# Linear attention ahead of two expert layers: one PSUM bank for both key-value sums, two for transposed queries

## The chip, the cores and the metric

The kernel runs as one launch on one core of a Trainium2 chip. The metric is the device time of a run in microseconds. The engines are TensorE (PE in the profile, with its weight loads as PEld), VectorE (DVE), ScalarE (ACT), GpSimd (POOL) and SyncE (SP), whose queue here only starts DMAs. They run on their own and wait for one another by semaphores. Each engine takes its instructions in the order in which the program wrote them.

## The reference, cut to what matters

```python
def phi(x):                                   # x: 8 x 8 x 576 x 64, w_phi: 64 x 128
    proj = x @ w_phi
    proj = proj - np.max(np.abs(proj), axis=-1, keepdims=True)
    return np.concatenate([np.exp(proj), np.exp(-proj)], axis=-1)      # 256 features
q_p, k_p = phi(q), phi(k)
kv  = k_p^T v                                  # per head: 256 x 64, summed over 576 positions
z   = sum of k_p over the positions            # per head: 256
out = (q_p @ kv) / (q_p . z + 1e-6)
x   = moe(out)          # gated layer, 4608 x 512 through 1536
y   = moe2(x)           # routed layer, 8 experts
```

The weights of the gated layer arrive as 64-bit floats, which the kernel turns into 32-bit floats by integer operations on their two halves.

## The kernel before, in words

Three stages follow each other: attention (up to about 363 us of the trace), the gated layer (up to about 1290 us) and the routed layer. Only the first and the weight conversion change.

**Units and ticks.** Attention works on 16 units. A unit is four heads, as two pairs (`pr` 0 and 1) of two heads each; the two heads of a pair share the 128 partitions or the columns of a matmul. The 576 positions of the two pairs together make nine blocks of 128, taken in three chunks `j` of three blocks. Block 0 is shared: its lower 64 rows belong to pair 0 and its upper 64 to pair 1. The function `attention` is a loop over ticks `tau`, three for each unit; in each tick it writes the steps of several units in a fixed order. `at(f, tau, off)` runs step `f` for the chunk `tau - off`; `once(f, tau, off, ..)` runs it once for the unit that started `off` ticks before. This order, written by hand, is the order of every engine's queue.

**The steps.** `proj` multiplies a chunk of k or q by `w_phi` into PSUM (`ppk`, `ppq`: two banks each, one buffer each). `shift` on VectorE takes the maximum of the absolute values (L94) and subtracts it (L96), into `kpm` or `qpm`. `k_exp` on ScalarE makes both exponentials `kE` (L102). `kv_mm` (L122) sums v times kE into `kv`. `z_add` on GpSimd adds blocks of kE (L133 to L139), and `z_mm` (L144) sums the rest over the partitions with a matrix of ones. `kv_out` copies the sums to SBUF (`kvf`, L147), `kv_tr` (L153) transposes them and copies them back as `KV` (L154). `q_trL` (L159) and `q_tr` (L172) transpose the shifted queries (`lt`, `qt`), `q_exp` (L181) makes their exponentials `qE`, and `q_num` (L193, `nu`) and `q_den` (L212, `dn`) multiply them with KV; `q_out` (L199) and `den_out` (L217) copy and store the results.

**PSUM.** All eight banks are in use: four for `ppk` and `ppq`, one for pair 0's `kv` and `kt`, one for pair 1's, one for `lt` and `qt`, and one for `nu` and `dn`.

**The conversion.** `to_f32` (L306) loads 512 KB and gives two functions. `one` is three VectorE instructions: clear the sign (L317), clamp (L318), shift and mask (L319). `two` is two more (L322, L323). In attention one conversion of `win` (24 in all) takes two ticks: `one` at the end of a tick's work and `two` at the end of the next. In the gated layer 12 conversions of `wout` are written ahead of the split of each weight chunk, one or two in a pass.

**The hand-over.** `START` and `K_TICKS` say at which ticks the first pieces of the gated layer are written between attention's last ones.

Of the kernel before, what the change touches and what calls it, by code (L numbers as in the profile page):

```python
# [10 lines left out]
F32 = mybir.dt.float32  # L11
# [3 lines left out]
AF = mybir.ActivationFunctionType  # L15
ALU = mybir.AluOpType
# [3 lines left out]
B, H, S, D = 8, 8, 576, 64  # L20
F = 128
N = B * S
DM = H * D
NU = 16
P = 128
# [4 lines left out]
GT = 3  # L30


K_TAGS = ("k", "kpm", "kE", "z", "v")
K_TICKS = 3 * NU + 2


def phi_constants(nc, pool, wphi):
# [9 lines left out]
def attention(kctx, qctx, tc, K, wphi, qT, kT, vT, num_d, den_d, r_d, units=NU, extra=None):  # L47
# [3 lines left out]
    nc = tc.nc  # L51
    V, A, G, PE = nc.vector, nc.scalar, nc.gpsimd, nc.tensor
# [3 lines left out]
    psq = qctx.enter_context(tc.tile_pool(name="psq", bufs=1, space=PSUM, side="right"))  # L56
    ident = K["ident"]
    K["qp"] = qp
    w, ones = phi_constants(nc, qp, wphi)
    X = {}  # L60

    def T(shape, dt, tag, key, bufs):
        pool = kp if tag in K_TAGS else qp
        t = pool.tile([P, *shape], dt, tag=tag, bufs=bufs, name=tag + "_".join(map(str, key)))
        X[(tag, *key)] = t
        return t
# [2 lines left out]
        nc.sync.dma_start(T([GT * P], F32, tag, (u, j), 3), src[u, :, j * GT * P : (j + 1) * GT * P])  # L69

    def load_v(u, j):
        t = T([GT, 2, D], F32, "v", (u, j), 4)
        nc.sync.dma_start(t.rearrange("p n h d -> p (n h d)"), vT[u, :, j * GT * P : (j + 1) * GT * P])

    def proj(tag, u, j):
# [27 lines left out]

    def kv_mm(u, j):

        v, E = X["v", u, j], X["kE", u, j]
        todo = [[(0, t, slice(0, P)) for t in (1, 2)], [(0, 0, slice(0, P)), (0, 1, slice(0, P))], []][j]
        if j == 0:
            todo.insert(0, (0, 0, slice(0, D)))
        else:  # L110
            todo += [(1, t, slice(0, P)) for t in ((2,) if j == 1 else range(GT))]
        if j == 1:
            todo.append((1, None, slice(D, P)))
        for i, (pr, t, r) in enumerate(todo):
            start = (j, i) == (0, 0) or (j, i) == (1, 2)
            stop = (j, i) == (1, 1) or (j, i) == (2, GT - 1)
            if start:
                X["kv", u, pr] = psq.tile([P, 3, P], F32, tag=f"kv{pr}", bufs=1, name=f"kv{u}_{pr}")
            v1, E1 = (X["v", u, 0][r, 0], X["kE", u, 0][r, 0]) if t is None else (v[r, t], E[r, t])
            for hh in range(2):  # L120
                o = X["kv", u, pr][64 * hh : 64 * hh + 64, 0:2].rearrange("p s f -> p (s f)")
                PE.matmul(o, lhsT=v1[:, hh], rhs=E1[:, hh].rearrange("p s f -> p (s f)"), start=start, stop=stop)  # L122

    def z_add(u, pr, i):

        def e(j, t):
            return X["kE", u, j][:, t].rearrange("p h s f -> p (h s f)")

        if i == 0:
            z = T([2, 4 * F], F32, "z", (u, pr), 2)  # L130
            r = slice(64 * pr, 64 * pr + 64)
            a, b = ((0, 1), (0, 2)) if pr == 0 else ((2, 0), (2, 1))
            G.tensor_tensor(z[:, 0], e(*a), e(*b), op=ALU.add)  # L133
            G.tensor_tensor(z[r, 0], z[r, 0], e(0, 0)[r], op=ALU.add)
        else:
            z = X["z", u, pr]
            a, b = ((1, 0), (1, 1)) if pr == 0 else ((1, 2), (2, 2))
            G.tensor_tensor(z[:, 1], e(*a), e(*b), op=ALU.add)
            G.tensor_tensor(z[:, 1], z[:, 0], z[:, 1], op=ALU.add)  # L139

    def z_mm(u, pr):
        z, kv = X.pop(("z", u, pr)), X["kv", u, pr]
        for c in range(4):
            PE.matmul(kv[32 * c : 32 * c + 32, 2], lhsT=ones, rhs=z[:, 1, c * F : (c + 1) * F], start=True, stop=True)  # L144

    def kv_out(u, pr):
        A.activation(T([3, P], F32, "kvf", (u, pr), 2), X.pop(("kv", u, pr)), AF.Copy)  # L147

    def kv_tr(u, pr):
        kt = psq.tile([P, 3, P], F32, tag=f"kv{pr}", bufs=1, name=f"kt{u}_{pr}")  # L150
        f = X.pop(("kvf", u, pr))
        for i in range(3):
            PE.transpose(kt[:, i], f[:, i], ident)  # L153
        A.activation(T([3, P], F32, "KV", (u, pr), 3), kt, AF.Copy)  # L154

    def q_trL(u):
        lt = psq.tile([P, 2, P], F32, tag="qt", bufs=1, name=f"lt{u}")
        for hh in range(2):
            PE.transpose(lt[:, hh], X["qpm", u][:, 0, hh], ident)  # L159
        X["lt", u] = lt  # L160
# [6 lines left out]

    def q_tr(u, h):
        pr, hh = h // 2, h % 2
        tp = psq.tile([P, 4, P], F32, tag="qt", bufs=1, name=f"qt{u}_{h}")  # L170
        for j in range(4):
            PE.transpose(tp[:, j], X["qpm", u][:, 1 + 4 * pr + j, hh], ident)  # L172
        X["qt", u, h] = tp
# [29 lines left out]

    def q_den(u, pr):
        KV = X["KV", u, pr]
        dn = psq.tile([P, 288], F32, tag="nu", bufs=1, name=f"dn{u}_{pr}")
        for s in range(2):
            for c in range(4):
                r = slice(32 * c, 32 * c + 32)
                z = 32 * (2 * (c // 2) + s)  # L210
                e = X["qE", u, 2 * pr + c // 2][:, s, 288 * (c % 2) : 288 * (c % 2) + 288]
                PE.matmul(dn[r], lhsT=KV[:, 2, z : z + 32], rhs=e, start=s == 0, stop=s == 1)  # L212
        X["dn", u, pr] = dn
# [21 lines left out]
    def at(f, tau, off, *pre):  # L235

        u, j = divmod(tau - off, 3)
        if 0 <= u < units:
            f(*pre, u, j)

    def once(f, tau, off, *post):
        u, j = divmod(tau - off, 3)
        if 0 <= u < units and j == 0:
            f(u, *post)

    for tau in range(-2, 3 * units + 6):
        at(load, tau, -2, kT, "k")
        at(load, tau, 0, qT, "q")
        at(load_v, tau, -1)

        once(q_out, tau, 7, 2)
        once(den_out, tau, 6, 0)
        once(den_out, tau, 8, 1)
        once(kv_out, tau, 3, 0)
        once(kv_out, tau, 5, 1)

        once(q_trL, tau, 3)
        once(q_tr, tau, 4, 0)
        once(q_tr, tau, 5, 2)
        once(q_expL, tau, 3)  # L260
        once(q_exp, tau, 4, 0)
        once(q_exp, tau, 5, 2)
        at(proj, tau, 0, "k")
        at(proj, tau, 2, "q")
        at(shift, tau, 0, "k")
        at(shift, tau, 2, "q")
        once(kv_tr, tau, 3, 0)
        once(kv_tr, tau, 5, 1)
        once(q_tr, tau, 4, 1)
        once(q_tr, tau, 5, 3)  # L270
        once(q_exp, tau, 4, 1)
        once(q_exp, tau, 5, 3)
        once(z_add, tau, 1, 0, 0)
        once(z_add, tau, 2, 0, 1)
        once(z_add, tau, 3, 1, 0)
        once(z_add, tau, 3, 1, 1)

        once(q_num, tau, 5, 0)
        once(q_num, tau, 6, 1)
        once(q_num, tau, 7, 3)  # L280
        once(q_out, tau, 5, 0)
        once(q_out, tau, 6, 1)
        once(q_out, tau, 7, 3)
        at(kv_mm, tau, 1)
        once(q_num, tau, 6, 2)
        at(k_exp, tau, 0)

        once(z_mm, tau, 2, 0)
        once(z_mm, tau, 4, 1)
        once(q_den, tau, 5, 0)  # L290
        once(q_den, tau, 7, 1)
        once(lambda u: recip_load(u // 2) if u % 2 and u + 1 < units else None, tau, 9)
        once(lambda u: recip(u // 2) if u % 2 and u + 1 < units else None, tau, 11)
        if extra is not None:
            extra(tau)
        yield tau
# [9 lines left out]
def to_f32(nc, pool, src, dst, name):  # L306

    V = nc.vector
    w = pool.tile([P, 512, 2], I32, tag="dbl", name=f"dbl{name}")
    nc.sync.dma_start(w.rearrange("p a b -> p (a b)"), src.bitcast(I32))  # L310

    lo, hi = w[:, :, 0], w[:, :, 1]
    a = dst.bitcast(I32)
    af = a.bitcast(F32)

    def one():
        V.tensor_scalar(a, hi, 0x7FFFFFFF, None, op0=ALU.bitwise_and)  # L317
        V.tensor_scalar(af, af, 2.0**-15, F64_MAX, op0=ALU.max, op1=ALU.min)  # L318
        V.tensor_scalar(a, a, 3, 0x3FFFFFF8, op0=ALU.logical_shift_left, op1=ALU.bitwise_and)  # L319

    def two():
        V.scalar_tensor_tensor(a, hi, -(1 << 30), a, op0=ALU.bitwise_and, op1=ALU.bitwise_or)  # L322
        V.scalar_tensor_tensor(a, lo, 29, a, op0=ALU.logical_shift_right, op1=ALU.bitwise_or)  # L323

    return one, two
# [879 lines left out]

START = (K_TICKS - 5, K_TICKS, K_TICKS, K_TICKS + 1, K_TICKS + 2)
NAMES = ["qT", "kT", "vT", "wphi", "win", "wout", "wg2", "w1", "w2"]
# [3 lines left out]
def attention__moe__moe2_kernel(ctx, tc, qT, kT, vT, wphi, win, wout, wg2, w1, w2, out):  # L1211
# [29 lines left out]
    with tc.manual_schedule():  # L1241
        main, rows = ffn(fctx, tc, K, num_d, r_d, wos_d, wout, wg2, w1, w2, wlo_d, x2_d, L, free)
        for tau in attention(kctx, qctx, tc, K, wphi, qT, kT, vT, num_d, den_d, r_d, extra=convert):
            if tau == K_TICKS:
                assert not todo and not late
# [34 lines left out]
```

## Time and profile before

| | us |
|---|---|
| median of 3 runs | 1817.92 (1817.77 to 1820.62) |
| profiled execution, its own time | 1814.72 |
| its span, first to last instruction | 1813.0 |
| TensorE busy in the span | 1747.5 (96%) |
| VectorE busy | 1270.3 (70%) |
| ScalarE busy | 577.1 (32%) |
| GpSimd busy | 525.3 (29%) |

The mean granted clock of TensorE is 0.987 of full speed. Matmuls overlap, so that the busy time of TensorE is larger than what its matmuls take one after the other: the distance between the starts of two groups is the better price. A row of the timeline that ends in brackets tells how long the engine had sat idle and what ended it.

### The profile page before, as it was taken

What the parts mean: (1) busy time and instruction counts of PE and PEld (TensorE: products, weight loads), DVE (VectorE), ACT (ScalarE), POOL (GpSimd) and SP (SyncE); (2) the same over time, 40 slices, a digit from 0 to 9 for tenths busy, and PEclk for the clock granted to TensorE, in tenths of its full rate; (3) what the DMA queues carried; (4) which work ended last, traced back from release to release, by engine and by line L of the source; (5) the groups of instructions that cost most, each with busy time, mean ns of one, the idle gap of its engine ahead of it and who ended that gap; (6) DMA issues with size and microseconds to landing.
All of it is one profiled execution on the core that took longest, in us unless ns stands there. A gap on an engine that the chain in (4) does not pass through costs nothing.

```text
span 1813.0 us, 32696 instructions
## 1 busy us (share of the span) xinstructions
PE 1747.5 (96%) x11900; PEld 1477.1 (81%) x11900; DVE 1270.3 (70%) x2999; ACT 577.1 (32%) x1112; POOL 525.3 (29%) x461
## 2 busy tenths in 40 slices
PE   7999999899999999999999999999989999999997
PEld 5666656577999999999999999997677889878886
DVE  7999998788768567686776855736757776777410
ACT  4666666622122222222222221111132333233331
POOL 5555555444122223222233221001112211210221
PEclk8999999999999999999999999999989999999999
DMA  4545444375666676666677664201364554465652
GB/s 141 165 150 160 142 142 144 116 245 186 224 230 225 220 238 218 235 220 221 219 243 231 201 227 147 79 1 40 126 198 148 198 195 166 158 198 162 213 171 80
DMA packets 174289, 318.30 MB, mean 176 GB/s; under 512 B 22704, under 2 KB 53680, under 8 KB 174000
## 3 DMA queue, kind: packets, MB, share of 16 engines
q1 hardware_dynamic: 144624, 254.33, 44.1%
q10 hardware_dynamic: 23616, 43.00, 6.3%
q0 software_dynamic: 5888, 18.88, 3.0%
q8 instruction: 94, 1.54, 0.3%
q14 instruction: 67, 0.55, 0.1%
HBM read 244.53 MB, written 71.60 MB: 174 GB/s over the span
## 4 chain that ended last, share of the span: by engine, by line
PE 69%; DVE 4%; DMA 1%; issue 1%; ACT 0%; SPq 0%; POOLq 0%; DVEq 0%; ACTq 0%
PE pg L398 30%; PE acc L420 15%; PE hp L1080 12%; PE yp L1114 8%; PE yr L1101 1%; PE tp L1053 1%; PE cnt L801 1%; DVE cmp L780 1%; DMA rb<-r_d 0%; DMA xg<-x_d,idx 0%; PE lg L454 0%; PE warm L670 0%; PE num_ix L996 0%; DVE oa L987 0%; DMA wos_d<-wh 0%
## 5 line engine op out<-in xcount | busy, mean ns | idle before, releaser
L398 PE MATMUL pg<-xl,wh 128*128 128x384 f32 x1152 | 389.3, 338 | 0.0
L398 PE MATMUL pg<-xh,wl 128*128 128x384 f32 x1152 | 388.0, 337 | 0.0
L398 PE MATMUL pg<-xh,wh 128*128 128x384 f32 x1152 | 386.8, 336 | 0.0
L547 POOL TENSOR_TENSOR el<-er,eh 128x512 fp32r<-128x512 f32 x128 | 183.0, 1429 | 467.9 <-ACT eh L546 410.8
L401 ACT ACTIVATE sg<-pg 128x384 f32<-128x384 f32 x144 | 70.6, 490 | 535.1 <-PE pg L398 510.1
L407 DVE TENSOR_TENSOR sg<-sg,pg 128x384 f32<-128x384 f32 x132 | 72.9, 552 | 239.0 <-PE pg L398 234.4
L398 PEld LDWEIGHTS pg<-xh,wh 128*128 128x128 f32 x1152 | 217.0, 188 | 7.7 <-issue 0.9
L398 PEld LDWEIGHTS pg<-xh,wl 128*128 128x128 f32 x1152 | 215.9, 187 | 5.3
L398 PEld LDWEIGHTS pg<-xl,wh 128*128 128x128 f32 x1152 | 216.4, 188 | 0.0
L478 DVE SCALAR_TENSOR_TENSOR junk<-x,wg 128x512 f32<-128x512 f32 x240 | 194.5, 810 | 5.6
L420 PE MATMUL acc<-wh,gh 128*128 128x512 f32 x396 | 159.6, 403 | 4.7 <-DVE gh L414 2.5
L420 PE MATMUL acc<-wl,gh 128*128 128x512 f32 x396 | 157.8, 398 | 2.2 <-POOL wl L436 2.2
L420 PE MATMUL acc<-wh,gl 128*128 128x512 f32 x396 | 158.3, 400 | 1.3 <-DVE gl L415 1.2
L1114 PE MATMUL yp<-wh,hh 128*128 128x512 f32 x256 | 108.1, 422 | 0.0
L546 ACT ACTIVATE eh<-er 128x512 fp32r<-128x512 f32 x128 | 81.0, 633 | 73.5 <-POOL el L547 41.2
L1114 PE MATMUL yp<-wl,hh 128*128 128x512 f32 x256 | 100.1, 391 | 0.0
L1114 PE MATMUL yp<-wh,hl 128*128 128x512 f32 x256 | 100.1, 391 | 0.0
L1087 DVE SCALAR_TENSOR_TENSOR hl<-hp,hh 128x288 fp32r<-128x288 f32 (+1 forms) x128 | 54.0, 422 | 60.2 <-ACT hh L1085 60.0
L1080 PE MATMUL hp<-xhT,wh 128*128 128x288 f32 x512 | 93.9, 305 | 0.8 <-ACT xhT L1055 0.8
L1080 PE MATMUL hp<-xhT,wl 128*128 128x288 f32 x512 | 94.3, 301 | 0.0
L420 PEld LDWEIGHTS acc<-wh,gl 128*128 128x128 f32 x396 | 75.2, 190 | 21.4 <-DVE gl L415 3.8
L420 PEld LDWEIGHTS acc<-wh,gh 128*128 128x128 f32 x396 | 75.3, 190 | 17.9 <-issue 3.5
(261 smaller groups left out, 3278.8 us busy)
## 6 DMA issues: line engine op xcount, KB each, us to landing
er<-in_w_dram SPq DMA_DIRECT2D x128, 256.0 KB
wlo_d<-el ACTq DMA_DIRECT2D x128, 256.0 KB
wr<-in_w_dram SPq DMA_DIRECT2D x128, 256.0 KB
wl<-wlo_d SPq DMA_DIRECT2D x128, 256.0 KB
wh<-wos_d SPq DMA_DIRECT2D x120, 256.0 KB
wl<-wos_d SPq DMA_DIRECT2D x120, 256.0 KB
dbli<-in_win_dram SPq DMA_DIRECT2D x24, 512.0 KB
k<-in_kT_dram SPq DMA_DIRECT2D x48, 192.0 KB
```

What stands on the lines that cost most here:

```text
L398: PE.matmul(pg, lhsT=a[:, cc], rhs=b, start=c == 0 and j == 0, stop=c == 3 and j == 2)
L401: A.activation(T([TB], F32, "sg", (g,)), X.pop(("pg", g, 0)), AF.Sigmoid)
L407: V.tensor_tensor(u, sg, X.pop(("pg", g, 1)), op=ALU.mult)
L420: PE.matmul(X["acc", i][t], lhsT=a[:, c], rhs=b, start=f == 0 and j == 0, stop=f == NF - 1 and j == 2)
L478: V.scalar_tensor_tensor(junk, x, 1.0, X["wg"][:, e], op0=ALU.mult, op1=ALU.mult, accum_out=out)
L546: A.activation(h, r, AF.Copy)
L547: G.tensor_tensor(tile("el", F32R, k - 1, 3), r, h.bitcast(F32), op=ALU.subtract)
L780: V.tensor_tensor(t[:, c], d[:, c, None, :].to_broadcast([P, NC // 4, NT, 2]), K["it2"][:, None, 0:P:4].to_broadcast([P, NC // 4, NT, 2]), ...
L801: PE.matmul(cnt[:, : 4 * E8], lhsT=eq[:, c // 2 : c // 2 + 2].rearrange("p c t b -> p (c t b)"), rhs=oh[:, c : c + 4].rearrange("p c e -> ...
L1080: PE.matmul(hp, lhsT=x[:, cc], rhs=y[:, c, s], start=c == 0 and j == 0, stop=c == 3 and j == 2)
L1087: V.scalar_tensor_tensor(hl[:, s], hs, 0.0, hh[:, s].bitcast(F32), op0=ALU.max, op1=ALU.subtract)
L1114: PE.matmul(yp, lhsT=x[:, cc], rhs=y, start=f == 0 and j == 0, stop=f == 7 and j == 2)
```

## The change

- Both pairs' key-value sums share one bank (`kv`), one after the other. Pair 1's sum is no longer begun in chunk 1: `kv_mm` for chunk 2 does all of it, out of v and kE of all three chunks, so that v is kept in 6 buffers and not 4.
- The bank that this frees gives `lt` and `qt` two buffers. Pair 0's `dn` is put there too, and no longer waits for the bank of `nu`.
- The transpositions stand together: `kv_tr`, then both `q_tr` of the pair. The queries' projection comes one tick earlier (offset 1, not 2), the rest of the queries' work and pair 1's sums follow one tick earlier, and `K_TICKS` is one less.
- `z_add` no longer adds its two partial sums on GpSimd: three additions a pair, not four. `z_mm` adds them in PSUM, with eight matmuls a pair, not four.
- The sign is cleared on ScalarE, as an absolute value (new L310, `AF.Abs`), not on VectorE. VectorE's next instruction waits for it.

```diff
-K_TICKS = 3 * NU + 2
+K_TICKS = 3 * NU + 1
...
+        pr = j // 2
+        full, half = slice(0, P), slice(pr * D, pr * D + D)
+        todo = [(0, 0, half)]
+        todo += [[(0, t, full) for t in (1, 2)], [(1, t, full) for t in (0, 1)], [(1, 2, full)] + [(2, t, full) for t in range(3)]][j]
+        if j == 1:
+            todo.pop(0)
...
+            X["kv", u, pr] = psq.tile([P, 3, P], F32, tag="kv", bufs=1, name=f"kv{u}_{pr}")
...
-            G.tensor_tensor(z[:, 1], e(*a), e(*b), op=ALU.add)
-            G.tensor_tensor(z[:, 1], z[:, 0], z[:, 1], op=ALU.add)
...
-        for c in range(4):
-            PE.matmul(kv[32 * c : 32 * c + 32, 2], lhsT=ones, rhs=z[:, 1, c * F : (c + 1) * F], start=True, stop=True)
+        for i in range(2):
+            for c in range(4):
+                o = kv[32 * c : 32 * c + 32, 2]
+                PE.matmul(o, lhsT=ones, rhs=z[:, i, c * F : (c + 1) * F], start=i == 0, stop=i == 1)
...
-        tp = psq.tile([P, 4, P], F32, tag="qt", bufs=1, name=f"qt{u}_{h}")
+        tp = psq.tile([P, 4, P], F32, tag="qt", bufs=2, name=f"qt{u}_{h}")
...
-        dn = psq.tile([P, 288], F32, tag="nu", bufs=1, name=f"dn{u}_{pr}")
+        tag, bufs = ("nu", 1) if pr else ("qt", 2)
+        dn = psq.tile([P, 288], F32, tag=tag, bufs=bufs, name=f"dn{u}_{pr}")
...
-        at(proj, tau, 2, "q")
+        at(proj, tau, 1, "q")
...
-        V.tensor_scalar(a, hi, 0x7FFFFFFF, None, op0=ALU.bitwise_and)
+        nc.scalar.activation(af, hi.bitcast(F32), AF.Abs)
```

In the rows below a name carries unit and part: `qt2_3` is the fourth transposition of unit 2, `kE3_1` is chunk 1 of unit 3, `win0_2` a weight chunk.

On TensorE, before, from the end of one tick into the next, around the transposition of pair 1's sums of unit 2:

```order
L172 MATMUL qt2_2_921<-ident_66,qpm2_691 128x128 x4
L81 MATMUL ppk3_2_930<-wphi2_160,k3_2_747 128x128 x6
L81 MATMUL ppq3_0_937<-wphi2_160,q3_0_749 128x128 x6
L153 MATMUL kt2_1_952<-ident_66,kvf2_1_919 128x128 x3
L172 MATMUL qt2_3_958<-ident_66,qpm2_691 128x128 x4
```

and now:

```order
L120 MATMUL kv2_1_859<-kE2_2_764,v2_2_625 64x256 x6
L141 MATMUL kv2_1_859<-z2_1_848,ones_158 32x128 x8
L81 MATMUL ppk3_1_892<-wphi2_160,k3_1_707 128x128 x6
L81 MATMUL ppq3_0_899<-wphi2_160,q3_0_709 128x128 x6
L150 MATMUL kt2_1_914<-ident_66,kvf2_1_890 128x128 x3
L169 MATMUL qt2_2_920<-ident_66,qpm2_648 128x128 x4
L169 MATMUL qt2_3_925<-ident_66,qpm2_648 128x128 x4
```

The transposition that stood ahead of the projections stands behind them, and only the two projections stand between the last matmuls on the sums and their transposition.

On VectorE, before, over two ticks (a conversion's first three and last two instructions behind the shifts):

```order
L96 TENSOR_TENSOR qpm2_691<-ppq2_1_774,mq_2_1_785 128x2x3x128
L317 TENSOR_SCALAR win0_2_121<-dbli2_0_745 128x512
L318 TENSOR_SCALAR win0_2_121<-win0_2_121 128x512
L319 TENSOR_SCALAR win0_2_121<-win0_2_121 128x512
L94 TENSOR_REDUCE mk_3_1_854<-ppk3_1_840 128x6
```

and now:

```order
L96 TENSOR_TENSOR qpm2_648<-ppq2_2_810,mq_2_2_821 128x2x3x128
L311 TENSOR_SCALAR win0_2_121<-win0_2_121 128x512
L312 TENSOR_SCALAR win0_2_121<-win0_2_121 128x512
L94 TENSOR_REDUCE mk_3_1_906<-ppk3_1_892 128x6
L96 TENSOR_TENSOR kpm3_1_907<-ppk3_1_892,mk_3_1_906 128x2x3x128
```

One of the three is gone, and L311 now waits for ScalarE.

On ScalarE, before, from the end of a tick's exponentials to the next copy of the sums:

```order
L199 ACTIVATE nums2_0_969<-nu2_0_970 128x288
L102 ACTIVATE kE3_2_985<-kpm3_2_945 128x6x128 x2
L217 ACTIVATE den2_0_1010<-dn2_0_992 128x288
L147 ACTIVATE kvf3_0_1016<-kv3_0_880 128x384
L166 ACTIVATE eL3_1021<-lt3_1018 128x256 x2
```

and now:

```order
L102 ACTIVATE kE3_0_870<-kpm3_0_818 128x6x128 x2
L310 ACTIVATE win0_2_121<-dbli2_0_786 128x512
L144 ACTIVATE kvf2_1_890<-kv2_1_859 128x384
L151 ACTIVATE KV2_1_918<-kt2_1_914 128x384
L178 ACTIVATE qE2_2_930<-qt2_2_920 128x512 x2
```

The absolute value stands right behind the exponentials of the chunk and ahead of the copy of the sums.

## Rows read from the trace of the kernel before

**Rows 1.** Stretches: us, length, busy of PE, PEld, DVE, ACT, POOL, clock, DMA.

```profile
100.00:150.00 50.00, 50.00 (x542) 31.74 (x542) 44.73 (x54) 33.54 (x66) 30.94 (x30) 1.00 0.50 152
150.00:200.00 50.00, 46.04 (x478) 29.37 (x474) 48.65 (x46) 29.67 (x58) 27.96 (x28) 0.97 0.47 145
```

**Rows 2.** Timeline of PE, once a unit: start us, us, instruction.

```profile
41.92 0.44 PE L159 MATMUL lt<-ident,qpm 128*128 128x128 f32 x2
...
81.69 0.44 PE L159 MATMUL lt<-ident,qpm 128*128 128x128 f32 x2
...
104.95 0.44 PE L159 MATMUL lt<-ident,qpm 128*128 128x128 f32 x2
...
124.83 0.44 PE L159 MATMUL lt<-ident,qpm 128*128 128x128 f32 x2
...
336.05 0.44 PE L159 MATMUL lt<-ident,qpm 128*128 128x128 f32 x2
```

**Rows 3.** Waits of PE from 50 to 340 us: total, times, longest.

```profile
PE qt L172 <- DVE qpm L96: 9.5, 7, 2.2
```

**Rows 4.** Timeline of PE at three places where it had waited.

```profile
25.82 0.69 PE L172 MATMUL qt<-ident,qpm 128*128 128x128 f32 x2 [2.84 <-DVE qpm L96]
...
195.09 0.44 PE L172 MATMUL qt<-ident,qpm 128*128 128x128 f32 x2 [2.17 <-DVE qpm L96]
195.46 1.34 PE L81 MATMUL ppk<-wphi,k 64*128 64x128 f32 x12
```

**Rows 5.** Timeline of DVE: a conversion undisturbed, then in a late tick.

```profile
122.83 0.42 DVE L317 TENSOR_SCALAR win<-dbli 128x512 int32<-128x512 int32 x1
...
164.16 1.53 DVE L317 TENSOR_SCALAR win<-dbli 128x512 int32<-128x512 int32 x1
165.72 1.38 DVE L318 TENSOR_SCALAR win<-win 128x512 f32<-128x512 f32 x1
...
168.43 0.94 DVE L94 TENSOR_REDUCE mk<-ppk 128x6 f32<-128x768 f32 x1
...
171.34 0.96 DVE L96 TENSOR_TENSOR qpm<-ppq,mq 128x768 f32<-128x768 f32 x1
```

**Rows 6.** Timeline of POOL beside the late conversion.

```profile
165.48 1.33 POOL L134 TENSOR_TENSOR z<-z,kE 64x512 f32<-64x512 f32 x1
```

**Rows 7.** Timeline of PE in a unit without waits.

```profile
116.14 0.43 PE L144 MATMUL kv<-z,ones 128*32 128x128 f32 x8
116.38 1.15 PE L212 MATMUL dn<-qE,KV 128*32 128x288 f32 x16
117.47 0.66 PE L172 MATMUL qt<-ident,qpm 128*128 128x128 f32 x4
118.06 0.94 PE L81 MATMUL ppk<-wphi,k 64*128 64x128 f32 x12
...
119.59 0.55 PE L153 MATMUL kt<-ident,kvf 128*128 128x128 f32 x3
119.98 0.60 PE L172 MATMUL qt<-ident,qpm 128*128 128x128 f32 x4
120.51 1.19 PE L193 MATMUL nu<-qE,KV 128*64 128x288 f32 x8
```

**Rows 8.** Groups by line and shape, 50 to 340 us: busy, mean ns, idle before.

```profile
L102 ACT ACTIVATE kE<-kpm 128x768 f32<-128x768 f32 x82 | 64.4, 835 | 17.8 <-DVE kpm L96 17.8
...
L317 DVE TENSOR_SCALAR win<-dbli 128x512 int32<-128x512 int32 x21 | 17.7, 841 | 0.0
...
L147 ACT ACTIVATE kvf<-kv 128x384 f32<-128x384 f32 x28 | 13.6, 485 | 0.0
```

**Rows 9.** Group of ACT in the gated layer, 340 to 1290 us.

```profile
L435 ACT ACTIVATE wh<-wo 128x512 fp32r<-128x512 f32 x12 | 7.6, 632 | 62.8 <-issue 41.1 <-DVE wo L323 21.6
```

**Rows 10.** Timeline of PE where attention ends and the gated layer goes on.

```profile
360.24 1.19 PE L193 MATMUL nu<-qE,KV 128*64 128x288 f32 x8 [1.40 <-ACT nums L199]
...
363.05 0.45 PE L398 MATMUL pg<-xh,wh 128*128 128x384 f32 x1
```

More of the change, by code (lines that the diff above doesn't have):

```diff
@@ L71, in load_v @@
     def load_v(u, j):
-        t = T([GT, 2, D], F32, "v", (u, j), 4)
+        t = T([GT, 2, D], F32, "v", (u, j), 6)
         nc.sync.dma_start(t.rearrange("p n h d -> p (n h d)"), vT[u, :, j * GT * P : (j + 1) * GT * P])
@@ L104, in kv_mm @@
     def kv_mm(u, j):
[L106 to L109, printed above, removed]
-        else:
[L111 to L119, printed above, removed]
+        pr = j // 2
[4 more added lines that the diff above has]
+            todo.pop(0)
+        else:
+            X["kv", u, pr] = psq.tile([P, 3, P], F32, tag="kv", bufs=1, name=f"kv{u}_{pr}")
+        for i, (g, t, r) in enumerate(todo):
+            v, E = X["v", u, g][r, t], X["kE", u, g][r, t]
             for hh in range(2):
                 o = X["kv", u, pr][64 * hh : 64 * hh + 64, 0:2].rearrange("p s f -> p (s f)")
-                PE.matmul(o, lhsT=v1[:, hh], rhs=E1[:, hh].rearrange("p s f -> p (s f)"), start=start, stop=stop)
+                e = E[:, hh].rearrange("p s f -> p (s f)")
+                PE.matmul(o, lhsT=v[:, hh], rhs=e, start=j != 1 and i == 0, stop=j > 0 and i == len(todo) - 1)
     def z_add(u, pr, i):
@@ L129, in z_add @@
         if i == 0:
-            z = T([2, 4 * F], F32, "z", (u, pr), 2)
-            r = slice(64 * pr, 64 * pr + 64)
[L132 to L137, printed above, removed]
-            G.tensor_tensor(z[:, 1], e(*a), e(*b), op=ALU.add)
-            G.tensor_tensor(z[:, 1], z[:, 0], z[:, 1], op=ALU.add)
+            T([2, 4 * F], F32, "z", (u, pr), 2)
+        z = X["z", u, pr][:, i]
+        a, b = (((0, 1), (0, 2)), ((1, 0), (1, 1)), ((2, 0), (2, 1)), ((1, 2), (2, 2)))[2 * pr + i]
+        G.tensor_tensor(z, e(*a), e(*b), op=ALU.add)
+        if i == pr:
+            r = slice(64 * pr, 64 * pr + 64)
+            G.tensor_tensor(z[r], z[r], e(0, 0)[r], op=ALU.add)
     def z_mm(u, pr):
         z, kv = X.pop(("z", u, pr)), X["kv", u, pr]
-        for c in range(4):
-            PE.matmul(kv[32 * c : 32 * c + 32, 2], lhsT=ones, rhs=z[:, 1, c * F : (c + 1) * F], start=True, stop=True)
+        for i in range(2):
+            for c in range(4):
+                o = kv[32 * c : 32 * c + 32, 2]
+                PE.matmul(o, lhsT=ones, rhs=z[:, i, c * F : (c + 1) * F], start=i == 0, stop=i == 1)
     def kv_out(u, pr):
@@ L149, in kv_tr @@
     def kv_tr(u, pr):
-        kt = psq.tile([P, 3, P], F32, tag=f"kv{pr}", bufs=1, name=f"kt{u}_{pr}")
+        kt = psq.tile([P, 3, P], F32, tag="kv", bufs=1, name=f"kt{u}_{pr}")
         f = X.pop(("kvf", u, pr))
@@ L156, in q_trL @@
     def q_trL(u):
-        lt = psq.tile([P, 2, P], F32, tag="qt", bufs=1, name=f"lt{u}")
+        lt = psq.tile([P, 2, P], F32, tag="qt", bufs=2, name=f"lt{u}")
         for hh in range(2):
@@ L247, in attention @@
         at(load, tau, -2, kT, "k")
-        at(load, tau, 0, qT, "q")
+        at(load, tau, -1, qT, "q")
         at(load_v, tau, -1)
-        once(q_out, tau, 7, 2)
+        once(kv_out, tau, 3, 0)
+        once(kv_out, tau, 4, 1)
+        once(q_out, tau, 6, 2)
         once(den_out, tau, 6, 0)
         once(den_out, tau, 8, 1)
[L254 to L262, printed above, removed]
         at(proj, tau, 0, "k")
-        at(proj, tau, 2, "q")
+        at(proj, tau, 1, "q")
         at(shift, tau, 0, "k")
-        at(shift, tau, 2, "q")
+        at(shift, tau, 1, "q")
         once(kv_tr, tau, 3, 0)
[L268 to L272, printed above, removed]
+        once(kv_tr, tau, 4, 1)
+        once(q_trL, tau, 2)
+        for h in range(2):
+            once(q_tr, tau, 3, h)
+            once(q_tr, tau, 4, 2 + h)
+        once(q_expL, tau, 2)
+        for h in range(2):
+            once(q_exp, tau, 3, h)
+            once(q_exp, tau, 4, 2 + h)
         once(z_add, tau, 1, 0, 0)
@@ L276, in attention @@
         once(z_add, tau, 3, 1, 1)
[L278 to L283, printed above, removed]
+        for off, i in ((4, 0), (5, 1), (6, 3)):
+            once(q_num, tau, off, i)
+            once(q_out, tau, off, i)
         at(kv_mm, tau, 1)
-        once(q_num, tau, 6, 2)
+        once(q_num, tau, 5, 2)
         at(k_exp, tau, 0)
         once(z_mm, tau, 2, 0)
-        once(z_mm, tau, 4, 1)
+        once(z_mm, tau, 3, 1)
         once(q_den, tau, 5, 0)
```

## The prediction

> **What bounds the kernel now.** I read the stretches of the span first, then TensorE's timeline in attention, then its waits, then VectorE beside GpSimd. From 100 to 150 us TensorE has no idle time and a full clock; from 150 to 200 it is busy for 46.04 of 50 us at 0.97, and VectorE, at 48.65, is then the fuller engine [rows 1]. So attention is bound by TensorE, and in some units by VectorE. The unit's first transposition shows how much: 104.95 to 124.83 is 19.88 us, a unit without waits; 81.69 to 104.95 is 23.26 [rows 2]. From 41.92 to 336.05 are 14 units and 294.1 us; 14 times 19.88 is 278.3, so 15.8 us are lost in the middle of attention. TensorE's waits there are all of one kind, 9.5 us in 7 pieces, for the shifted query of the tick before [rows 3]. The rest is clock: behind the wait at 195.09 twelve projection matmuls take 1.34 us and not 0.94 [rows 4, 7].
>
> Why VectorE is late is seen in one tick. Its four shift instructions take 168.43 to 172.30, 3.87 us. Ahead of them L317 took 1.53 us where the same instruction took 0.42 at 122.83, and L318 took 1.38 [rows 5]. GpSimd's addition ran from 165.48 to 166.81 and L318 ended at 167.10, 0.29 later [rows 5, 6]: the slow form is a wait for GpSimd. With all three instructions slow, a tick costs VectorE 3.87 + 1.53 + 1.4 + 1.4 (L319 taken at L318's price), 8.2 us, against TensorE's 19.88 / 3 = 6.63.
>
> **The change part by part.** The sum goes along TensorE up to the point where the gated layer runs without a break, at 363.05 [rows 10].
>
> *More matmuls for z.* A group of four (eight rows of the trace) moves the next group by 116.38 - 116.14 = 0.24 us [rows 7]. One more per pair is 0.48 a unit, all on the bounding engine. The ends are zero, if the second set hides in the first, and the group's whole 0.43 each, 0.86 a unit. I take 0.48, since the rows follow each other closely on one weight matrix.
>
> *Transpositions together.* Four of them take 118.06 - 117.47 = 0.59 us behind another kind of matmul, and 120.51 - 119.98 = 0.53 behind a transposition [rows 7]. Two groups a unit gain that, 0.12. The key-value matmuls are as many as before, ten blocks a unit, and only move; I cost that at nothing, between a gain and a loss of 0.2 a unit (a switch of kind, 0.06, three times). A unit is then 19.88 + 0.48 - 0.12 = 20.24 us, and 14 are 283.4.
>
> *The sign on ScalarE.* VectorE loses L317, 0.84 us in the mean [rows 8], 24 times in attention. In the late tick 8.2 becomes 3.87 + 2 x 1.4 = 6.7 us, about TensorE's new 20.24 / 3 = 6.75. So the loss that VectorE made should mostly go. But L311 now waits for ScalarE, where the absolute value stands behind the chunk's two exponentials (1.67 us) [rows 8]. Its own price isn't shown; a ScalarE copy of the same 128x512 takes 0.63 [rows 9], the 768-wide exponential 0.84, the 384-wide copy 0.49 [rows 8]. I take 0.63, so ScalarE finishes it 2.3 us after the key shift, when VectorE has just finished the query shift (1.9 us later). That alone costs VectorE 0.4 us a conversion; if ScalarE comes late to the exponentials, more. Queued behind L311 are the next tick's shifts, and TensorE's next projections and ScalarE's exponentials wait for those. What the order gives in return is a longer way: the transposition that TensorE waited at stands behind two projections now, 1.53 us later (119.59 - 118.06) [rows 7]. I leave 2.5 us of stalls in the 14 units, between none and the 15.8 of before, near the low end, because a tick of VectorE fits even with both instructions slow.
>
> By the Trainium skill (SBUF — State Buffer, Who interferes with whom) a VectorE instruction in a two-port mode and a GpSimd instruction lock each other out for a whole instruction, so the absolute value's place would make it worse: GpSimd starts its additions when the exponentials end, just ahead of L311. The trace agrees about the lock, by the 0.29 us above; by that rule alone both instructions would always be slow, and that is the first rival.
>
> *GpSimd.* It loses two of eight additions a unit (1.33 us each by the one shown [rows 6]), 2.7 us, off the path; less of it stands in VectorE's way. I count nothing further.
>
> *Banks.* Pair 1's sums must now wait until ScalarE has copied pair 0's transposed ones out of the one bank. By the new order two groups of transpositions and a `nu` group stand between on TensorE, about 2.2 us (0.53 + 0.53 + 1.19 [rows 7]), against one copy of 0.49 [rows 8]: hidden, if ScalarE is on time. Pair 0's `dn` no longer waits for ScalarE to empty `nu`. Only the new second rival counts these waits.
>
> *The ends.* One tick of depth goes. Behind the last unit's mark 27.0 us pass (363.05 - 336.05) [rows 2, 10]. The query's first transposition, two `nu` groups and part of a `kv` group now stand ahead of it, about 3.1 us of matmuls (0.44 [rows 2], two of 1.19 [rows 7], and 0.3 left to the `kv` group, an estimate), and the waits there (1.40 us at one of them [rows 10]) lose perhaps 1.4: 22.5. The bounds are 27.0 and a whole tick less, 20.4. At the head the same work comes earlier and falls into holes like the 2.84 us at 25.82 [rows 4]; VectorE has one more query shift there (1.9 us) and three L317 fewer (2.5). I take 40.4 for 41.92, between 38 and 44.
>
> *The gated layer.* Twelve conversions lose an L317 on VectorE, and ScalarE has room for them: it sat idle for 62.8 us ahead of the split's copy [rows 9]. Minus 0.5, between a gain of 2 and a loss of 2. The matmuls behind are the same.
>
> *Sum.* 40.4 + 283.4 + 2.5 + 22.5 = 348.8 against 363.05, 14.2 less; with the gated layer 14.7. The profiled execution took 1814.72 (span 1813.0), so 1800.0. The median of the runs shown is 3.2 above that execution, which gives 1803.
>
> **The rivals.**
>
> *VectorE stays late.* If GpSimd meets both instructions of every conversion, each costs about a microsecond more than its undisturbed 0.43, 24 times 1.9 or 46 us of VectorE's time, most of it inside the slack of 6.75 us ticks. If 0.35 us of each conversion reaches TensorE, 8 us of stall stand where I have 2.5: 1809. For it speaks that the starting signal is shared; against it, that GpSimd has a quarter less to add.
>
> *The one bank, and slower than before.* From the last z matmul to the transposition of the sums TensorE has only its two projections, 1.53 us [rows 7]. In that time ScalarE must copy the sums, 0.49, which leaves about 1.0. If ScalarE is then still at exponentials and absolute value (2.3 us), the copy is late by 1.3, TensorE stands, and nothing can fill another bank. At 24 conversions that is 31 us: 1834. It decides from 14.7 / 32 = 0.46 us at each of the 32 pairs. Against it: ScalarE is busy for only 33.5 of 50 us [rows 1], and pair 1's sums of ten blocks are long, so that it should have caught up.
>
> *No change to speak of.* If the second z set costs 0.43 and not 0.24, 16 units lose 6.1 us more, and if the ends gain nothing, 6 more: 1815.
>
> **How the numbers follow.** The forecast has 0.62, the late VectorE 0.17, the bank 0.11, no change 0.10. What a measurement of this kernel can tell from no change is about 0.2%, 3.6 us, so faster is under 1814.3 and slower over 1821.6. Faster: all of the forecast and nearly all of the first rival and a third of the last, 0.82. Same: 0.08. Slower: 0.10. The range goes from 1796 (no stalls, 2.5; head at 38, 2.4; a gated layer with 1.5 more gained) to 1815, the last rival; it leaves out the bank.
>
> **What would show it.** Right: unit marks 20.2 us apart at a clock of 1.00, two z sets 0.48 us long, no wait for the shifted query, the gated layer's second set of matmuls starting near 349 us, an absolute value near 0.63. Wrong: VectorE idle ahead of L311 by over a microsecond with TensorE waiting at a projection one tick later (first rival); TensorE waiting at `kt` for `kvf` or at `kv` for `KV` (second); marks over 20.6 us apart with no waits at all (third).

## The result and the profile after

The changed kernel takes 1799.18 us in the median (1794.65 to 1800.71, six runs) against 1819.03 for the kernel before in the same series: a ratio of 0.9888, 95% interval 0.9873 to 0.9904. The forecast was 1803, inside a range of 1796 to 1815. The profiled execution has a span of 1792.9 us where it was 1813.0, 20.1 less.

The page of the changed kernel, its first lines:

```profile
span 1792.9 us, 33156 instructions
...
PE 1738.4 (97%) x12156; PEld 1476.4 (82%) x12156; DVE 1250.4 (70%) x2963; ACT 593.5 (33%) x1148; POOL 479.5 (27%) x429
```

The same two stretches of attention as in [rows 1], after the change:

```profile
100.00:150.00 50.00, 50.00 (x578) 33.06 (x578) 46.47 (x47) 34.50 (x68) 25.08 (x26) 1.00 0.54 171
150.00:200.00 50.00, 50.00 (x578) 31.54 (x581) 46.82 (x49) 34.58 (x69) 20.78 (x23) 1.00 0.48 159
```

TensorE now has no hole in either, at a full clock. VectorE is nearly as full as before.

The timeline of TensorE with the marks that answer to [rows 2, 10]. The first transposition of a unit no longer opens a tick; the next tick begins 4.87 us behind it:

```profile
34.28 0.44 PE L156 MATMUL lt<-ident,qpm 128*128 128x128 f32 x2
...
39.15 0.94 PE L81 MATMUL ppk<-wphi,k 64*128 64x128 f32 x12
...
54.44 0.44 PE L156 MATMUL lt<-ident,qpm 128*128 128x128 f32 x2
...
316.87 0.44 PE L156 MATMUL lt<-ident,qpm 128*128 128x128 f32 x2
...
321.73 0.94 PE L81 MATMUL ppq<-wphi,q 64*128 64x128 f32 x12
...
342.35 1.19 PE L190 MATMUL nu<-qE,KV 128*64 128x288 f32 x8 [1.40 <-ACT nums L196]
...
346.87 0.44 PE L391 MATMUL pg<-xh,wh 128*128 128x384 f32 x1
```

A unit is 20.16 us long (54.44 - 34.28). The 14 units take 316.87 - 34.28 = 282.6, where they took 294.1: 11.5 less. The head, up to the tick of 41.92 in [rows 2], ends at 39.15: 2.8 less. At 346.87 the second set of the gated layer's matmuls (about 2.08 us) is done already, which began at 363.05 in [rows 10]; its counterpart is 344.8, so up to there 18.3 us are gained, and 18.3 - 11.5 - 2.8 = 4.0 of them in the tail. The other 1.8 of the 20.1 come later, in the gated layer's first 100 us, where the conversions of `wout` are. A second profile of the changed kernel, from a later run, gains as much up to there within 0.6 us, and yet its span is 1797.9 us: it loses 5 us in later stages that the change does not touch. So a gain is better read from such marks than from two spans.

Of the waits of TensorE from 50 to 340 us, that for the shifted query [rows 3] is gone. All but the last row here belong to the tail, behind the last unit's mark; the last one, for a load, makes one unit 20.52 us long:

```profile
PE nu L190 <- ACT den L215: 1.2, 1, 1.2
PE dn L210 <- ACT nums L196: 0.9, 1, 0.9
PE kt L150 <- ACT kvf L144: 0.7, 1, 0.7
PE nu L190 <- ACT nums L196: 0.5, 1, 0.5
PE ppk L81 <- DMA k<-in_kT_dram: 0.3, 1, 0.3
```

In a unit, against [rows 7], the groups that the change made longer or put together:

```profile
98.07 0.64 PE L141 MATMUL kv<-z,ones 128*32 128x128 f32 x16
98.53 1.15 PE L210 MATMUL dn<-qE,KV 128*32 128x288 f32 x16
...
101.15 0.55 PE L150 MATMUL kt<-ident,kvf 128*128 128x128 f32 x3
101.53 1.04 PE L169 MATMUL qt<-ident,qpm 128*128 128x128 f32 x8
102.50 1.19 PE L190 MATMUL nu<-qE,KV 128*64 128x288 f32 x8
```

Two z sets move the next group by 0.46 us (98.53 - 98.07), where one moved it by 0.24, and eight transpositions take 0.97 (102.50 - 101.53), where two groups of four took 0.59 and 0.53.

VectorE's and ScalarE's groups of the conversion, 50 to 340 us, against L317 in [rows 8]:

```profile
L316 DVE SCALAR_TENSOR_TENSOR win<-dbli,win 128x512 int32<-128x512 int32 x21 | 26.9, 1282 | 0.7
L315 DVE SCALAR_TENSOR_TENSOR win<-dbli,win 128x512 int32<-128x512 int32 x21 | 26.4, 1258 | 0.0
L312 DVE TENSOR_SCALAR win<-win 128x512 int32<-128x512 int32 x21 | 22.3, 1061 | 0.7
L311 DVE TENSOR_SCALAR win<-win 128x512 f32<-128x512 f32 x21 | 20.5, 978 | 17.2 <-ACT win L310 17.2
...
L310 ACT ACTIVATE win<-dbli 128x512 f32<-128x512 f32 x21 | 14.4, 686 | 0.9 <-DMA dbli<-in_win_dram 0.9
```

The four that are left still take 4.6 us, about twice what they take undisturbed (0.43, 0.43, 0.68 and 0.69 in the timeline): the clamp is slow in 19 of the 21 conversions and the shift in 14, each time beside an addition on GpSimd. VectorE also stands 17.2 us for the absolute value, which takes 0.69. It isn't seen in the time, since TensorE is the one that is never idle.

### The profile page after: what moved, and what is told of

It reads as the page before. It is cut to its first block, busy times and chain, and to the rows that moved or that the text cites. A ratio compares the mean times of both kernels' runs of the same rounds, so it can differ in the third digit from the quotient of the medians.

```text
span 1792.9 us, 33156 instructions
## 1 busy us (share of the span) xinstructions
PE 1738.4 (97%) x12156; PEld 1476.4 (82%) x12156; DVE 1250.4 (70%) x2963; ACT 593.5 (33%) x1148; POOL 479.5 (27%) x429
## 4 chain that ended last, share of the span: by engine, by line
PE 67%; DVE 6%; DMA 2%; issue 2%; ACT 1%; SPq 0%; POOLq 0%; POOL 0%; ACTq 0%; DVEq 0%
PE pg L391 29%; PE acc L413 14%; PE hp L1073 12%; PE yp L1107 8%; PE yr L1094 1%; PE tp L1046 1%; DMA rb<-r_d 1%; PE cnt L794 1%; DVE cmp L773 1%; DVE junk L471 1%; DVE oa L980 0%; DVE xn L364 0%; DMA xg<-x_d,idx 0%; PE lg L447 0%; DVE xh L367 0%
## 5 line engine op out<-in xcount | busy, mean ns | idle before, releaser
L471 DVE SCALAR_TENSOR_TENSOR junk<-x,wg 128x512 f32<-128x512 f32 x240 | 200.1, 834 | 5.5
L131 POOL TENSOR_TENSOR z<-kE 128x512 f32<-128x512 f32 x48 | 63.9, 1331 | 143.1 <-ACT kE L102 143.1
```

Source lines behind the costliest of these rows:

```text
L131: G.tensor_tensor(z, e(*a), e(*b), op=ALU.add)
L471: V.scalar_tensor_tensor(junk, x, 1.0, X["wg"][:, e], op0=ALU.mult, op1=ALU.mult, accum_out=out)
```

## The experiments

Theory A was the prediction's: TensorE waits where VectorE, held up by GpSimd, needs more than TensorE's tick, and the three parts (sign, z sums, order) each help a little. Its rivals were that the new order alone did it, and that GpSimd's relief alone did. So the change was cut into three: S, the sign on ScalarE; Z, the z sums on TensorE; O, the banks and the order. All eight combinations were measured, each against the kernel before on its own chip. A mark is the start of a unit's first transposition (`lt`), 0 to 15; the mean unit is the time from mark 1 to mark 15, in one profile, divided by 14.

| parts | ratio to before | 95% interval | mean unit, us |
|---|---|---|---|
| none | 1 | | 21.01 |
| S | 0.9976 | 0.9959 to 0.9994 | 20.87 |
| Z | 0.9935 | 0.9916 to 0.9955 | 20.33 |
| S, Z | 0.9915 | 0.9887 to 0.9943 | 20.33 |
| O | 1.0088 | 1.0059 to 1.0118 | 22.38 |
| S, O | 0.9944 | 0.9925 to 0.9963 | 21.00 |
| Z, O | 0.9990 | 0.9974 to 1.0006 | 21.39 |
| S, Z, O (the change) | 0.9888 | 0.9873 to 0.9904 | 20.19 |

### The change without one part, and the order alone

Without Z, on the changed kernel:

```diff
-        z = X["z", u, pr][:, i]
...
+            G.tensor_tensor(z[:, 1], z[:, 0], z[:, 1], op=ALU.add)
...
-        for i in range(2):
-            for c in range(4):
+        for c in range(4):
```

> The changed kernel with the partial z sums added on GpSimd again (four additions and four matmuls a pair). Theory A (VectorE was late because of GpSimd and L317; the z matmuls are a price paid on TensorE, 0.46 us a unit): units shorten from 20.16 to about 19.70 us where nothing waits, but GpSimd's two more additions a unit bring back about 3 us of TensorE's waits; about 1795. Rival B (the new order alone removed the waits): 19.70 in every unit, no waits, 16 x 0.46 = 7.4 us less: about 1792. If GpSimd's relief is what mattered: waits of 10 us or more come back and it is slower than the changed kernel, about 1803.

It takes 1806.1 us, 0.9944. From the third on the units alternate between 20.56 and 21.77. Waits of TensorE, 50 to 340 us:

```profile
PE ppq L81 <- DVE qpm L96: 9.6, 13, 1.3
PE ppk L81 <- DVE kpm L96: 1.8, 6, 0.3
```

That is the third of the three expectations, GpSimd's relief, and not mine. Without S:

```diff
-        nc.scalar.activation(af, hi.bitcast(F32), AF.Abs)
+        V.tensor_scalar(a, hi, 0x7FFFFFFF, None, op0=ALU.bitwise_and)
```

> The changed kernel with the sign cleared on VectorE again. Theory A: a tick with three slow instructions takes VectorE 8.2 us against TensorE's 6.72, so TensorE waits again, 5 to 8 us in the 14 units, now at the query's projection: about 1805. Rival B (order alone): no waits, units of 20.16, about 1799 as the changed kernel.

It takes 1813.36, 0.9990, with units of mostly 21.35 and 21.56. TensorE waits where theory A said:

```profile
PE ppq L81 <- DVE qpm L96: 8.2, 13, 0.8
```

But the loss is over twice what I had put down: 17 us in the 14 units (21.39 against 20.16) and not 5 to 8. With both edits, O alone:

> Only banks and order of the change; the sign on VectorE and the z sums on GpSimd as before. Theory A: units of 19.70 where nothing waits, but 8 to 12 us of waits and slow clock, so about 1800. Rival B: 19.70 throughout, about 1792, faster than the changed kernel.

It takes 1831.8, 1.0088. Both theories are far off: the order alone makes the kernel slower. The stretch from 50 to 340 us, TensorE's waits, and the conversion's groups on VectorE:

```profile
50.00:340.00 290.00, 266.92 (x2795) 165.23 (x2794) 282.07 (x264) 168.32 (x336) 160.46 (x156) 1.00 0.44 141
```

```profile
PE ppq L81 <- DVE qpm L96: 19.2, 24, 0.9
```

```profile
L316 DVE SCALAR_TENSOR_TENSOR win<-dbli,win 128x512 int32<-128x512 int32 x20 | 33.9, 1694 | 0.0
L317 DVE SCALAR_TENSOR_TENSOR win<-dbli,win 128x512 int32<-128x512 int32 x20 | 33.0, 1649 | 0.7
L311 DVE TENSOR_SCALAR win<-dbli 128x512 int32<-128x512 int32 x19 | 28.7, 1511 | 0.0
L312 DVE TENSOR_SCALAR win<-win 128x512 f32<-128x512 f32 x19 | 26.3, 1385 | 0.7
L313 DVE TENSOR_SCALAR win<-win 128x512 int32<-128x512 int32 x19 | 13.9, 729 | 0.7
```

VectorE is busy for 282 of 290 us: it bounds every unit. A conversion costs it 1.69 + 1.65 + 1.51 + 1.39 + 0.73 = 7.0 us. The timelines suggest why it does not get out of this state. VectorE, then GpSimd:

```profile
205.48 0.96 DVE L96 TENSOR_TENSOR qpm<-ppq,mq 128x768 f32<-128x768 f32 x1
206.36 1.47 DVE L311 TENSOR_SCALAR win<-dbli 128x512 int32<-128x512 int32 x1
207.86 1.38 DVE L312 TENSOR_SCALAR win<-win 128x512 f32<-128x512 f32 x1
```

```profile
206.28 1.27 POOL L131 TENSOR_TENSOR z<-kE 128x512 f32<-128x512 f32 x1 [2.02 <-ACT kE L102]
```

Where VectorE is late, ScalarE waits for its key shift, makes the exponentials (1.67 us by [rows 8]) and so releases GpSimd just when VectorE has done the query shift (1.9 us behind the key shift) and comes to the conversion: GpSimd's addition starts 0.08 us ahead of L311, and the conversion is late again. A late VectorE thus keeps itself late. Where TensorE or ScalarE is the late one, the exponentials and GpSimd start later, and part of the conversion is through by then, as in this unit of the kernel before, where L317 (0.42) and L318 are short:

```profile
136.49 0.43 DVE L318 TENSOR_SCALAR win<-win 128x512 f32<-128x512 f32 x1
136.50 1.54 POOL L138 TENSOR_TENSOR z<-kE 128x512 f32<-128x512 f32 x1 [2.58 <-ACT kE L102]
```

That this is the whole reason why O alone is slower, and not only what its trace shows, was not tried by itself.

### One or two parts in the old order

The edits are those of the change's diff: its last two lines for S, the lines of `z_add` and `z_mm` for Z.

> The kernel before with the sign on ScalarE alone. Theory A (in attention TensorE waits wherever VectorE, held up by GpSimd, needs more than TensorE's tick; each of the two reliefs counts): L317 was up to 1.5 of VectorE's 8.2 us, so 22 to 23 us units become 20 to 21, the mean about 20.3 with 4 to 7 us of waits left, about 1807. Rival (GpSimd's relief is the one that counts): units as before, within 0.2% of before.

S takes 1809.87, 0.9976. TensorE still waits 8.8 us for the shifted query, in ten pieces where it was 9.5 in seven [rows 3]:

```profile
PE qt L172 <- DVE qpm L96: 8.8, 10, 1.6
```

Neither expectation fits well. The time moved the way theory A says, but less; a mean unit of 20.87 and 8.8 us of waits are nearer to the rival's "as before" than to theory A's 20.3 and 4 to 7.

> The kernel before with the partial z sums added on TensorE alone. Theory A: two GpSimd additions fewer a unit leave VectorE half of its late ticks, so the 15.8 us of lost time fall to about 8, and the matmuls cost 16 x 0.46 = 7.4: within 0.2% of before, about 1815. Rival (GpSimd's relief is the one that counts): no waits, units of 20.3, about 1805.

Z takes 1802.64, 0.9935: the rival. Every unit is 20.32 or 20.33. TensorE waits for nothing from VectorE; the longest of its waits in the same stretch, and the conversion's groups:

```profile
PE qt L171 <- ACT qE L180: 0.7, 2, 0.4
```

```profile
L322 DVE SCALAR_TENSOR_TENSOR win<-dbli,win 128x512 int32<-128x512 int32 x21 | 29.8, 1418 | 0.7
L318 DVE TENSOR_SCALAR win<-win 128x512 int32<-128x512 int32 x21 | 26.1, 1243 | 0.7
L321 DVE SCALAR_TENSOR_TENSOR win<-dbli,win 128x512 int32<-128x512 int32 x21 | 17.3, 824 | 0.0
L317 DVE TENSOR_SCALAR win<-win 128x512 f32<-128x512 f32 x21 | 13.3, 632 | 0.7
L316 DVE TENSOR_SCALAR win<-dbli 128x512 int32<-128x512 int32 x21 | 9.4, 448 | 1.5 <-DMA dbli<-in_win_dram 1.5
```

A conversion is 4.6 us here, with the sign still on VectorE: L316, the sign, takes 0.45 where it took 0.84 [rows 8]. So the z sums on TensorE, which I had entered as a pure cost with nothing in return, remove all of TensorE's waits for VectorE in the old order. They do two things at once: GpSimd has two additions fewer, and TensorE's unit is 0.45 us longer, which is room for VectorE. No run parts the two.

> The kernel before with the sign on ScalarE and the z sums on TensorE, in the old order and banks. Theory A: VectorE is relieved, so most of the 15.8 us of lost time goes (12 to 13), while the z matmuls cost 7 more: about 1813. Rival B (the order did it): waits stay at 9 us or more and the z matmuls are added: about 1826.

S with Z takes 1800.85, 0.9915, faster than either theory said, and its units are those of Z alone. The order adds 0.14 us a unit and the ends: in the profiles the gated layer's first split of `wout` on ScalarE starts at 364.7 us without the order and at 356.2 with it, 8.5 earlier, of which 2.0 are units. The times bear this out less sharply, since the two intervals in the table overlap.

### One bank for the queries again

```diff
-            X["kv", u, pr] = psq.tile([P, 3, P], F32, tag="kv", bufs=1, name=f"kv{u}_{pr}")
+            X["kv", u, pr] = psq.tile([P, 3, P], F32, tag=f"kv{pr}", bufs=1, name=f"kv{u}_{pr}")
...
-        tp = psq.tile([P, 4, P], F32, tag="qt", bufs=2, name=f"qt{u}_{h}")
+        tp = psq.tile([P, 4, P], F32, tag="qt", bufs=1, name=f"qt{u}_{h}")
```

and the same for `kt`, `lt` and pair 0's `dn`.

> The changed kernel with two banks for the key-value sums again and one for the transposed queries; the order is the new one. Theory A (the bank pays for transpositions that stand together): each pair's second transposition waits until ScalarE has copied KV and made both exponentials of the first, about 1.2 us, twice a unit: units of about 22.5, about 1838. Rival (VectorE alone sets the units): TensorE's waits there are hidden in nothing but slack, units of 20.2 and about 1799.

It takes 1836.56, 1.0125 (1.0092 to 1.0158), with units of 22.95. Theory A, near its number. TensorE's timeline at such a wait, of which there are 25 from 50 to 340 us, 29.4 us in all:

```profile
202.53 0.60 PE L169 MATMUL qt<-ident,qpm 128*128 128x128 f32 x4
204.30 0.66 PE L169 MATMUL qt<-ident,qpm 128*128 128x128 f32 x4 [1.18 <-ACT qE L178]
```

So the second bank of the queries is what lets transpositions stand together, and one bank for the key-value sums costs nothing that shows. Two banks for the sums in the new order, with two for the queries, would need a ninth bank and weren't tried.

### Half of the z sums, and the sign ahead of the exponentials

Pair 1's partial sums go back to GpSimd, where the addition falls beside VectorE's work on PSUM, and pair 0's stay on TensorE:

```diff
+        if i == pr == 1:
+            G.tensor_tensor(z, X["z", u, 1][:, 0], z, op=ALU.add)
...
-        for i in range(2):
+        for i in range(pr, 2):
...
```

> The changed kernel with pair 1's two partial z sums added on GpSimd (seven additions a unit) and pair 0's on TensorE (twelve z matmuls a unit). Theory A: VectorE reads and writes PSUM while GpSimd does pair 1's last addition, so nothing is held up, and the units take 20.16 - 0.23 = 19.93: about 1795.5, with no waits. Rival (any more GpSimd work holds VectorE up): half of the way to the kernel with all z sums on GpSimd, units of about 20.6, slower than the changed kernel, about 1803.

It takes 1791.77, 0.9885 (0.9851 to 0.9918). The units are 19.94, and from the sixth on every second one 20.1 to 20.2. It was then run beside the changed kernel on one chip:

> The changed kernel itself, as the measure on this chip for the two others. All theories: 0.989 of before, about 1799.

> Pair 1's z sums added on GpSimd, pair 0's on TensorE, once more beside the changed kernel. Theory A (a z set is 0.23 us of a unit that TensorE bounds): 16 x 0.23 = 3.7 less, minus about 1 us for the 0.26 us by which every second unit came longer: 2.5 to 5 us faster than the changed kernel, about 1795. Rival: the same time as the changed kernel within a microsecond, since what TensorE saves comes back as waits.

The changed kernel took 1797.14, 0.9888 (0.9858 to 0.9918), and this one 1794.57, 0.9871 (0.9843 to 0.9898). The units with half of the z sums repeat to 0.03 us; the total differs by 2.6, as theory A has it, but the intervals overlap. For the longer second units the absolute value was written ahead of the chunk's exponentials:

```diff
+        if early is not None:
+            early()
         at(k_exp, tau, 0)
...
```

> As the kernel before it, and the absolute value written ahead of the chunk's exponentials on ScalarE, so that VectorE should not wait for it. Theory A (the 0.26 us in every second unit come from VectorE, which waits for the absolute value behind the exponentials): VectorE's wait of 9.7 us ahead of its clamp goes and all units take 19.93: about 1 us less than the kernel before it. Rival (ScalarE's exponentials then come 0.65 us later in every second tick, and TensorE or GpSimd waits for those): units of 20.1 or more, same or slower.

It takes 1793.57, 0.9855 (0.9827 to 0.9882). All units are 19.93 or 19.94, as theory A said; the time is the same within the noise. VectorE's wait for the absolute value falls from 9.7 us to 5.2 and does not go, but something larger happens. The stretch from 50 to 340 us with the absolute value behind the exponentials (the run before), and ahead of them:

```profile
50.00:340.00 290.00, 285.19 (x3160) 180.84 (x3157) 271.48 (x275) 201.32 (x396) 151.45 (x157) 1.00 0.46 152
```

```profile
50.00:340.00 290.00, 285.33 (x3171) 181.34 (x3170) 223.38 (x276) 200.81 (x398) 149.50 (x157) 1.00 0.47 152
```

VectorE's busy time falls by 48 us, from 271 to 223, though it runs the same instructions. Clamp and shift are now through before the exponentials end and start GpSimd; they bring about 25 of the 48 (0.42 and 0.47 us in the mean, where the run before has 1.04 and 1.06). The conversion's other two instructions bring some 16 more and the small addition to the denominators (`dens`) 6, since they too are slow less often. Clamp and shift on VectorE's timeline:

```profile
104.52 0.43 DVE L320 TENSOR_SCALAR win<-win 128x512 f32<-128x512 f32 x1 [0.62 <-ACT win L316]
104.98 0.43 DVE L321 TENSOR_SCALAR win<-win 128x512 int32<-128x512 int32 x1
```

With that much room, all z sums were put back on GpSimd, with the sign ahead:

> The changed kernel with all z sums added on GpSimd again and the absolute value written ahead of the exponentials. Theory A (clamp and shift meet GpSimd only because the absolute value stood behind the exponentials, which start GpSimd too; with it ahead VectorE has 60 us of 290 to spare): the units that took 20.6 and 21.8 with it behind take 19.70 throughout, without waits; 0.983 to 0.985 of before. Rival (GpSimd's eight additions a unit hold VectorE's other two instructions up enough): units of 20 or more and waits for the shifted query, 0.987 or more of before.

It takes 1790.47, the lowest median here, on another chip; 0.9891 (0.9858 to 0.9923), an interval that overlaps those of the others. Ten of the units are 19.72, without waits, as theory A said; the five before them are 19.7 to 21.8. From 50 to 340 us TensorE's last wait for VectorE is this one:

```profile
110.32 0.94 PE L81 MATMUL ppq<-wphi,q 64*128 64x128 f32 x12 [0.92 <-DVE qpm L96]
```

So in this profile both held, one after the other: until about 110 us VectorE is in the late state, and then it is out of it and stays out. What moved it out the trace doesn't tell. By the ratio it is the rival's 0.987 or more and not theory A's 0.983 to 0.985. The closest comparison is with the kernel without Z, which differs from this one in the absolute value's place alone: 0.9944 (0.9925 to 0.9963) there and 0.9891 (0.9858 to 0.9923) here. These intervals lie just apart, so there the place alone is worth about half a per cent. Which of the last three is fastest the times don't tell; by the 14 units it is the half with the sign ahead (279.1 us, against 279.9 for this one, 280.5 with the sign behind and 282.6 for the change).

## Why the prediction was right, and where it was not

- **What bounds attention.** Right. TensorE bounds it at 19.88 us a unit, and VectorE wherever GpSimd holds it up. Each of the eight combinations is one of these two: a mean unit of 20.2 to 20.3 and no wait for VectorE (Z; S with Z; the change), or of 20.9 to 22.4 with such waits (the other five).
- **The z matmuls.** Right: 0.48 was said and 0.46 a unit is measured, and units without waits differ by 0.44 with Z and without (20.16 against 19.72).
- **Transpositions together.** A unit of 20.24 was said, 20.16 measured. The order was to save 0.12 of it; units without waits are 19.72 with it and 19.88 without, 0.16.
- **Stalls.** 2.5 us were left, and 0.35 are there, the one wait for a load. Here the size came out inside its bounds and the reason did not. "I count nothing further", the step on GpSimd, is the one that failed: its two additions fewer are what ends the waits in the old order (Z, 20.33 throughout), and the step that I gave the credit, the sign on ScalarE, brings 0.14 us a unit by itself (S, 20.87). In the new order the sign does count, 1.2 us a unit (21.39 to 20.19), so that part of the credit is right only there.
- **"What the order gives in return is a longer way."** It gave nothing by itself. The transposition no longer waits for the shifted query, but the wait moved to the queries' projection, 19.2 us in the order alone. With the other two parts undone, the order makes every unit VectorE's, 22.4 us in the mean. With the absolute value where the change puts it, both S and Z are needed to get out: with one of them the units are still 21.0 and 21.4.
- **The first rival.** Its lock is there: clamp and shift meet GpSimd in most conversions of the changed kernel, 19 and 14 of 21. Its price was not, because VectorE fits into the tick all the same, with 261.4 us busy and 17.2 us waiting of 290. The waiting is 0.82 us a conversion, where I had 0.4.
- **The bank.** The slower rival did not occur; `kt` waits for `kvf` once, 0.7 us, in the tail.
- **The ends.** Head: 1.5 less was said, 2.8 measured. Tail: 4.5 said, 4.0 measured. The gated layer: 0.5 said, 1.8 measured, inside its bounds.

In medians 1803 was said and 1799.18 measured. The sum was 14.7 and became 20.1: 3.3 more from the units (2.2 from stalls, 1.1 from the price of a unit), 1.3 from the head, 1.3 from the gated layer, less 0.5 in the tail.

## What to carry to other kernels

When an engine is late because another holds it up, look for what starts the other one: if the late engine's own result starts it, lateness can feed itself. Moving the short step ahead of the signal can then be worth as much as moving work away: in the new order without Z the first gave a ratio of 0.9891 and the second, the change itself, 0.9888. Parts of a change that look like a cost on the bounding engine can pay by what they take off a third engine, so cost an edit on every engine that it touches, and cut the change into its parts before giving one of them the credit. An order that helps a bound engine may hurt while another one bounds, as the order alone did here.

## What the runs showed of the hardware

VectorE and GpSimd hold each other up by whole instructions. A 128x512 clamp takes 0.42 us alone and up to 1.55 beside GpSimd. In the traces of the kernel before, of the change and of the order alone, from 50 to 340 us, every conversion instruction of VectorE that took over 0.95 us ended at a fixed distance behind the end of an addition on GpSimd: 0.28 or 0.29 us for those with one input, 0.55 for those with two. The other way round, an addition that GpSimd began during one of VectorE's conversion instructions ended 1.12 to 1.16 us behind that one's end, as at 136.50 above, 1.54 us long where undisturbed ones take 1.27. VectorE's shifts, which read PSUM, take 0.95 and 0.96 us in the mean in the kernel before and in the order alone alike. The same program with the same instructions had VectorE busy for 271 or 223 of 290 us depending only on where a third engine's instruction stood. The Trainium skill (SBUF — State Buffer, Who interferes with whom) states this lock for two-port modes, and that instructions with two inputs in SBUF contend with GpSimd's reads. The traces agree as far as they go: the two-input L316 and L317 of the order alone take 1.69 and 1.65 us, and the one-input clamp behaves as the Trainium skill says of a two-port mode, though no view names an instruction's mode. I had not expected that it gives the whole program two states, of 19.7 and of up to 21.8 us a unit, between which one execution changed at about 110 us.
